# A first transform without its two zero columns, coupled ticks in the first pair, an earlier identity load, and evictions shared 5 to 4

## The chip, the cores and the metric

The kernel runs on one core of one Trainium2 chip. The metric is device time in microseconds (us), from the start of an execution to its end. Before the change the median of three runs is 385.36 us (384.66 to 386.22).

The names of the profile are used throughout: PE is the matrix engine, PEld its weight loads, DVE the vector engine, ACT the scalar engine, POOL and SP the two engines that here mostly issue DMAs. ps is PSUM, the memory that PE writes to, in eight banks of 512 float32 columns.

## The reference

Two layers follow each other. The first is a causal long convolution of x (8 x 5696 x 128) with h (5696 x 128) along the sequence, by FFT of twice the length; the second keeps 64 Fourier modes of the result, mixes their channels with a complex 128 x 128 matrix per mode, goes back, adds that to its input, and adds a ReLU of a 128 x 128 product:

```
Xf = np.fft.rfft(x, n=2*S, axis=1);  Hf = np.fft.rfft(h, n=2*S, axis=0)
x  = np.fft.irfft(Xf * Hf, n=2*S, axis=1)[:, :S, :]
X  = np.fft.rfft(x, axis=1)
Yr = einsum('bmd,mde->bme', Xr, w_r) - einsum('bmd,mde->bme', Xi, w_i)
Yi = einsum('bmd,mde->bme', Xr, w_i) + einsum('bmd,mde->bme', Xi, w_r)
u  = x + np.fft.irfft(Y, n=S, axis=1)
return u + np.maximum(u @ w_ch, 0.0)
```

## The kernel before

All transforms are matrix products on PE. The sequence of 5696 is cut into J = 64 columns of NQ = 89 rows, and NK = 90 frequencies k (0 to 89) come out of the first transform. The batch is worked in four pairs (g_ = 0 to 3, two sequences each).

**Order of the work.** Nothing is scheduled by a planner: a recorder writes the instructions of each engine down in the order of the calls in the source, and puts in the semaphore waits that the named tokens call for (reads, writes, and an extra list, `after`). So each engine, and each DMA queue, works strictly in the source's order, and whatever stands behind a waiting instruction of its queue waits too.

**First transform (`a_tile`, tiles j = 0 to 31).** Each tile takes four channels: four matmuls of a 128 x 128 slice of Xin against the constant F (f1_sb, 180 columns: real and imaginary part of each of the 90 frequencies). Their output, 4 x 180 float32 columns, fills two banks and is evicted to As (a_sb) with a scale, by DVE (line 317) or ACT (line 313). In As the group 2k + r of 128 columns holds the real (r = 0) or imaginary (r = 1) part of frequency k. The imaginary parts of k = 0 and of k = 89 are zero, and so are two columns of F, columns 1 and 179. h goes through the same transform once, in 16 tiles, into Ah.

For the first pair the 32 tiles are evicted by ACT and DVE in turn, with a filter tick of h between some of them; there are four PSUM slots of two banks. For the later pairs tiles 0 to 5, the border tiles, stand inside the last ticks of the pair before (`border`), and tiles 6 to 31 follow as a run: even tiles on ACT, odd ones on DVE, and tile 31 in halves, one on each engine. Matmuls of F with itself (`keep`, and 92 before the first tile) stand where PE would have nothing to do.

**Ticks.** A pair then has 23 ticks t of four frequencies (the last has two), numbered s in what follows when a later stage of the same tick is meant. For tick t, `second(t)` does the second transform, 16 matmuls of 64-row slices of As against M (k by k; real part, then imaginary part), into a slot of two banks. `products(t)` lets ACT copy the slot to Xs and DVE multiply it by the filter Hs into U (in the later pairs, for t = 3, 7, 11 and so on, DVE reads PSUM itself and ACT has no copy to make). Two ticks later four matmuls with the constants W1, W2 (`Wc`, 512 columns each) make Z, in two of three PSUM banks (4, 5 and 6), which ACT evicts to a slot Zs (or Zt); SP stores the slot to the DRAM scratch zscr, and a tick later short matmuls with G take the modes out of it. In the last pair the store and the modes of tick s use the z slot s for s below 10, and then slots 0 to 7 again: ticks 13 and 21 have slot 3, ticks 14 and 22 slot 4. ACT may write a slot again only when the store of its earlier tick has landed.

In pairs 1 to 3 an odd tick issues `second(t)` and `second(t + 1)` together (`twin`), a couple, and the work on PE is then: 32 matmuls of the second transform, Z, G, Z, G. In pair 0 each tick stands alone. Ticks 0 to 16 of pair 0 also carry the filter's second transform, six ticks ahead (`filter_tick`, LH = 6).

**Last stage.** During the ticks of pair 3, `early` issues loads on the POOL queue for the last stage: the mixing weights W, ZT0 to ZT3 (pieces of zscr), the constants S4a, S4b and IBs. After tick 14 it also issues one on SP: `load_id`, the 32 KB identity Id, which goes to memory that z slots 8 and 9 of the last pair use, so that it waits for these slots (`after=ZY`), their stores included. When the ticks are over, `u_z` does the first 16 matmuls of the inverse transform (ZT0 with S4a and S4b), `mix` does 128 small matmuls with W (16 columns each), the result is turned with eight transposes that read Id (line 824), and from then on inverse transforms (`u_tile`), the product with w_ch, ReLU, addition and stores alternate until the end.

Of the kernel before, what the change touches and what calls it, by code (L numbers as in the profile page):

```python
# [4 lines left out]
P = 128  # L5
# [118 lines left out]
def bass_long_conv_fft__then__afno_spectral_mix_kernel(nc, x, h, moe_w_r, moe_w_i, moe_w_ch, out):  # L124
# [3 lines left out]
    J = 64  # L128
# [13 lines left out]
    f1 = np.zeros((P, 2 * NK))  # L142
    f1[0:NQ] = np.stack([fwd.real, fwd.imag], axis=2).reshape(NQ, 2 * NK)
# [105 lines left out]
    f1_sb = at("F1", 2 * NK, F16, take(2 * NK * 2))  # L249
# [13 lines left out]
    assert 2 * S + 8 * ZP <= AW * 2  # L263
# [19 lines left out]
    id_sb = at("Id", P, F16, r_off[1])  # L283
# [63 lines left out]
    R.add("scalar", lambda e: e.copy(zf, ap(f1_sb, 2 * NK, J, P - J, 1, [[0, XW // 2]])), [("f1",)], [("xz",)])  # L347
# [69 lines left out]
    dma("sync", wc_sb[:, :], bass.AP(c_w, 0, [[3 * P, P], [1, 2 * P]]), "c", (), [("wc",)])  # L417

# [13 lines left out]
    for i in range(WARM):  # L432
        mm(pv(6 + i % 2, 0, [[1, 2 * NK]]), f1_sb[:, 0:P], f1_sb[:, :], True, True, [("f1",)], [bank(6 + i % 2)])
# [6 lines left out]
    for j in range(16):  # L440
        t = turns("h", [0, 2, 4])
        for i in range(4):
            d = 4 * j + i
            mm(pv(t + i // 2, (i % 2) * 2 * NK, [[1, 2 * NK]]),
               ap(hp_sb, 2 * J * HS, 0, P, d, [[HS, 2 * J]]), f1_sb[:, :], True, True,
               [("hz",), ("hp", d // DC), ("f1",)], [bank(t + i // 2)])
        for i in range(4 if j < 15 else 26):
            mm(pv(6 + i % 2, 0, [[1, 2 * NK]]), f1_sb[:, 0:P], f1_sb[:, :], True, True, [("f1",)], [bank(6 + i % 2)])
        evac(bass.AP(ah_sb, 4 * j, [[HW, P], [DH, 2 * NK], [2, 2], [1, 2]]),
             pv(t, 0, [[1, 2 * NK], [512, 2], [2 * NK, 2]]),  # L450
             [bank(t), bank(t + 1)], [("ah", j)], 1.0 / 64,
             eng="vector" if j in (3, 7) else "scalar")
        if j % 2:
            i = j // 2 % 2 * XC + j // 4
            x_place(i, bass.AP(x_all, i * XB, [[RA, NQ], [D, XN], [1, D]]), XR[i])
# [5 lines left out]
    def a_tile(j, slots, eng=None):  # L461
        t = turns("s", slots) if len(slots) > 1 else slots[0]
        for i in range(4):
            d = 4 * j + i
            mm(pv(t + i // 2, (i % 2) * 2 * NK, [[1, 2 * NK]]),
               ap(x_sb, XW, 0, P, d, [[XS, 2 * J]]), f1_sb[:, :], True, True,
               XIN + XZ + [("f1",)], [bank(t + i // 2)])
        if eng == "both":
            for i, e in enumerate(("vector", "scalar")):
                evac(bass.AP(a_sb, 4 * j + 2 * i, [[AW, P], [D, 2 * NK], [1, 2]]), pv(t + i, 0, [[1, 2 * NK], [2 * NK, 2]]),  # L470
                     [bank(t + i)], [("as", j + i)], 1.0 / 64, eng=e, after=once(("hp", j), HP))
            return
        evac(bass.AP(a_sb, 4 * j, [[AW, P], [D, 2 * NK], [2, 2], [1, 2]]),
             pv(t, 0, [[1, 2 * NK], [512, 2], [2 * NK, 2]]),
             [bank(t), bank(t + 1)], [("as", j)], 1.0 / 64, eng=eng, after=once(("hp", j), HP))


# [8 lines left out]
    def filter_tick(t, banks):  # L486
        n = len(ticks[t])
        hb = banks
        for i, k in enumerate(ticks[t]):
            for r in range(2):  # L490
                for dh in range(2):
                    mm(pv(hb[dh], i * DH, [[1, DH]]),
                       ap(m_sb, MW, J * dh, J, k * 3 * J + (J if r == 0 else 0) + dh * J, [[1, P]]),
                       ap(ah_sb, HW, J * dh, J, (2 * k + r) * DH, [[1, DH]]), r == 0, r == 1,
                       AHT + mtok(k) + [("ag", k)], [bank(hb[dh])])
# [54 lines left out]
    def load_s4(part):  # L550
# [9 lines left out]
             14: lambda: (load_id(), clear_zt(1)),  # L560
# [7 lines left out]
    def load_id():  # L568
        dma("sync", id_sb[:, :], bass.AP(c_w, 2 * P, [[3 * P, P], [1, P]]), "c", (), [("id",)], after=ZY)

# [4 lines left out]
    def keep(n, b0):  # L575
        for i in range(n):
            mm(pv(b0 + i % 2, 0, [[1, 2 * NK]]), f1_sb[:, 0:P], f1_sb[:, :], True, True, [("f1",)], [bank(b0 + i % 2)])
# [17 lines left out]
    def twin(g_, t):  # L595
        return g_ > 0 and t % 2 == 1
# [9 lines left out]
    def second(g_, t):  # L606
        sl = slot_of(g_, t)
        for i, k in enumerate(ticks[t]):
            for r in range(2):
                for b in range(2):  # L610
                    col = k * 3 * J + (J if r == 0 else 0) + b * J
                    mm(pv(sl + b, i * D, [[1, D]]),
                       ap(m_sb, MW, J * b, J, col, [[1, P]]),
                       ap(a_sb, AW, J * b, J, (2 * k + r) * D, [[1, D]]), r == 0, r == 1,
                       AST + mtok(k), [bank(sl + b)])
# [100 lines left out]
    FOUR = [0, 2, 4, 6]  # L716
    for j in range(32):
        a_tile(j, FOUR)
# [4 lines left out]
    for g_ in range(NP):  # L723
# [15 lines left out]
        if g_ + 1 < NP:  # L739
            for j in range(6, 32):  # L740
                a_tile(j, [(4, 6, 0, 2)[(j - 7) % 4] if j > 6 else 0], "both" if j == 31 else V if j % 2 else A)
# [99 lines left out]
    def o_tile(g_, b, r4):  # L841
# [29 lines left out]
        R.add("scalar", lambda e: e.activation(rv, src_r, RELU), bk, [("r", i % NR)], after=once(("r", i % NR), G_ALL + XTT + [("y", 0), ("y", 1), ("id",)]))  # L871
# [67 lines left out]
```

## Time and profile before

| | |
|---|---|
| Median of three runs | 385.36 us (384.66 to 386.22) |
| The profiled execution's own time | 387.21 us |
| Its span, first to last instruction | 385.1 us |
| PE / DVE / ACT / POOL busy | 362.4 / 296.6 / 314.3 / 85.2 us |
| Mean granted clock of PE | 0.98 |
| DMA | 103.94 MB, mean 270 GB/s |

Stages of the span, from a table of windows:

| us from the span's start | work |
|---|---|
| 0 to 27.1 | h and x loaded, h transformed |
| 27.1 to 43.5 | 32 tiles of pair 0 |
| 43.5 to 90.3 | ticks of pair 0 (from 81.4 on ticks 17 to 22, without the filter) |
| 90.3 to 106.8 | end of pair 0's ticks with border tiles, then the run of tiles 6 to 31 of pair 1 |
| 106.8 to 217.6 | the same for pairs 1 and 2, with their successors' tiles (145.8 to 162.2, 201.3 to 217.6) |
| 217.6 to 262.8 | ticks of pair 3 |
| 262.8 to 274.1 | start of the last stage: inverse transform, mix, transposes |
| 274.1 to 385.1 | the last stage |

A row of the table of instruction groups or of the timeline gives a start, a length, the engine, the source line, what it writes and reads, the shape and how many were merged; the part in brackets is the idle time before it and what ended it. Merged rows let the distance from one start to the next be worked out, which is shorter than the duration of one instruction, since the ends of instructions overlap with the next one's start. The chain of waits is read from the end of the execution back: at every step it goes to what released the instruction. PEclk is the share of its clock that PE was granted.

### The profile page before, as it was taken

What the parts mean: (1) busy time and instruction counts of PE and PEld (TensorE: products, weight loads), DVE (VectorE), ACT (ScalarE), POOL (GpSimd) and SP (SyncE); (2) the same over time, 40 slices, a digit from 0 to 9 for tenths busy, and PEclk for the clock granted to TensorE, in tenths of its full rate; (3) what the DMA queues carried; (4) which work ended last, traced back from release to release, by engine and by line L of the source; (5) the groups of instructions that cost most, each with busy time, mean ns of one, the idle gap of its engine ahead of it and who ended that gap; (6) DMA issues with size and microseconds to landing.
All of it is one profiled execution on the core that took longest, in us unless ns stands there. A gap on an engine that the chain in (4) does not pass through costs nothing.

```text
span 385.1 us, 12438 instructions
## 1 busy us (share of the span) xinstructions
PE 362.4 (94%) x5346; PEld 280.7 (73%) x5346; DVE 296.6 (77%) x336; ACT 314.3 (82%) x491; POOL 85.2 (22%) x134
## 2 busy tenths in 40 slices
PE   7989899999989999999999899978999999999994
PEld 7878766667856667756667666648789989888873
DVE  3649899988988998989999988761537767766665
ACT  8469699898989997899998899965447777688884
POOL 8812012100733311823203213307200000000000
PEclk9999999999999999999999999995799999999999
DMA  7999969977999995999995799999999999999877
GB/s 148 206 298 354 243 139 249 250 220 222 97 126 215 249 268 151 132 134 232 243 274 114 95 325 357 327 367 292 392 391 362 367 416 403 419 405 383 325 293 316
DMA packets 87137, 103.94 MB, mean 270 GB/s; under 512 B 22819, under 2 KB 72611, under 8 KB 83527
## 3 DMA queue, kind: packets, MB, share of 16 engines
q1 hardware_dynamic: 62603, 67.76, 50.7%
q0 software_dynamic: 24480, 35.40, 44.2%
q8 instruction: 42, 0.69, 0.7%
q14 instruction: 12, 0.10, 0.1%
HBM read 70.61 MB, written 51.12 MB: 316 GB/s over the span
## 4 chain that ended last, share of the span: by engine, by line
PE 76%; DMA 8%; DVE 6%; ACT 4%; POOL 3%; issue 2%; DVEq 0%; ACTq 0%; POOLq 0%
PE ps L323 76%; DMA Xr<-in_x_dram 4%; DMA zscr<-Zs 3%; DVE As L317 2%; DVE U L630 2%; POOL Xr L320 2%; ACT As L313 2%; ACT R L871 1%; POOL Hin L320 1%; DVE Xin L365 1%; DVE Hs L315 1%; ACT Zt L311 1%; ACT Zs L311 0%; DMA Hs<-Hs 0%; ACT Xs L311 0%
## 5 line engine op out<-in xcount | busy, mean ns | idle before, releaser
L323 PE MATMUL ps<-U,Wc 128*128 128x512 f16 (+1 forms) x368 | 94.4, 377 | 4.2 <-ACT Zs L311 3.7
L638 DVE TENSOR_TENSOR U<-Xs,Hs 128x2048 f16<-128x2048 f16 (+1 forms) x73 | 86.9, 1192 | 13.8 <-ACT Xs L311 13.1
L311 ACT CAST Xs<-ps 128x1024 f16<-128x1024 f32 (+1 forms) x77 | 75.1, 979 | 12.6 <-PE ps L323 7.6
L311 ACT CAST Zs<-ps 128x512 f16<-128x512 f32 (+1 forms) x132 | 69.3, 592 | 5.5 <-DMA zscr<-Zs 3.8
L872 DVE TENSOR_TENSOR O<-ps,R 128x512 f32<-128x512 f32 x81 | 52.3, 685 | 20.1 <-ACT R L871 11.2
L317 DVE TENSOR_SCALAR As<-ps 128x720 f16<-128x720 f32 x70 | 57.7, 886 | 5.2 <-PE ps L323 4.6
L871 ACT ACTIVATE R<-ps 128x512 f32<-128x512 f32 (+1 forms) x92 | 50.5, 591 | 8.5 <-PE ps L323 8.4
L323 PE MATMUL ps<-F,Xin 128*128 128x180 f16 x512 | 53.7, 249 | 3.9 <-DVE Xin L365 2.6
L323 PE MATMUL ps<-As,M 64*128 64x128 f16 x1440 | 50.3, 217 | 3.5 <-DVE U L630 2.9
L323 PEld LDWEIGHTS ps<-F,Xin 128*128 128x128 f16 x512 | 44.4, 155 | 12.6 <-DVE As L317 2.8
L323 PEld LDWEIGHTS ps<-U,Wc 128*128 128x128 f16 x368 | 28.6, 97 | 33.3 <-ACT Zs L311 7.6
L313 ACT ACTIVATE As<-ps 128x720 f16<-128x720 f32 (+1 forms) x61 | 45.7, 769 | 7.9 <-PE ps L323 6.5
L323 PE MATMUL ps<-WI,UT 128*128 128x256 f16 x360 | 51.1, 278 | 0.5 <-ACT UT L311 0.4
L311 ACT CAST UT<-ps 128x712 f16<-128x712 f32 x46 | 34.5, 752 | 19.2 <-PE ps L323 18.0
L323 PEld LDWEIGHTS ps<-As,M 64*128 64x128 f16 x1440 | 40.6, 94 | 9.7 <-DVE U L630 3.6
L323 PEld LDWEIGHTS ps<-WI,UT 128*128 128x128 f16 x360 | 39.1, 152 | 3.4 <-issue 1.8
L323 PE MATMUL ps<-IBs,C 128*128 128x356 f16 x128 | 40.3, 324 | 0.1
L320 POOL DMA_DIRECT2D Xt<-in_x_dram x40 | 21.1, 533 | 80.8 <-PE ps L323 80.3
L323 PEld LDWEIGHTS ps<-G,Zs 128*128 128x128 f16 x512 | 26.3, 97 | 14.3 <-ACT Zs L311 1.6
L638 DVE TENSOR_TENSOR U<-ps,Hs 128x2048 f16<-128x2048 f32 x15 | 34.3, 2284 | 0.0
L323 PE MATMUL ps<-G,Zs 128*128 128x128 f16 (+2 forms) x512 | 32.4, 193 | 0.0
L311 ACT CAST Zt<-ps 128x512 f16<-128x512 f32 x52 | 28.5, 624 | 0.3 <-PE ps L323 0.3
(88 smaller groups left out, 504.7 us busy)
## 6 DMA issues: line engine op xcount, KB each, us to landing
out_dram<-O SPq DMA_DIRECT2D x39, 512.0 KB, 7.6
zscr<-Zs SPq DMA_DIRECT2D x62, 256.0 KB, 7.0
zscr<-Zt SPq DMA_DIRECT2D x26, 256.0 KB, 6.8
Xt<-in_x_dram POOLq DMA_DIRECT2D x20, 320.0 KB, 7.1
W<-wscr POOLq DMA_DIRECT2D x4, 1024.0 KB, 8.2
M<-cM POOLq DMA_DIRECT2D x5, 720.0 KB, 16.9
ZT0a<-zscr SPq DMA_DIRECT2D x3, 1024.0 KB, 8.8
Hs<-Hs SPq DMA_DIRECT2D x44, 64.0 KB, 6.3
```

Source lines behind the costliest of these rows:

```text
L311: R.add(e, lambda h_: h_.copy(dst, src), reads, writes, after=after)
L313: R.add(e, lambda h_: h_.activation(dst, src, COPY, scale=scale), reads, writes, after=after)
L315: R.add(e, lambda h_: h_.tensor_copy(dst, src), reads, writes, after=after)
L317: R.add(e, lambda h_: h_.tensor_scalar_mul(dst, src, scale), reads, writes, after=after)
L320: R.add(eng, lambda h_: h_.dma_start(dst, src), reads, writes, ring=ring, after=after)
L323: R.add("tensor", lambda h_: h_.matmul(o, l, r, start=st, stop=sp), reads, writes)
L365: R.add("vector", lambda e: e.tensor_copy(bass.AP(x_sb, i * XN * XS, [[XW, NQ], [XS, XN], [1, D]]), src), list(toks) + XZ, [("xin", i)])
L630: R.add("vector", lambda e, b=b, s_=s_: e.tensor_tensor(bass.AP(u_s[i], b * 512, [[2048, P], [1024, 2], [1, n * D]]), s_, hv, MULT), [tok, ...
L638: R.add("vector", lambda e: e.tensor_tensor(uv, src, hv, MULT), bk + [("h", t, 0), ("h", t, 1, 0), ("h", t, 1, J)], [("u", i)])
L871: R.add("scalar", lambda e: e.activation(rv, src_r, RELU), bk, [("r", i % NR)], after=once(("r", i % NR), G_ALL + XTT + [("y", 0), ("y", 1 ...
L872: R.add("vector", lambda e: e.tensor_tensor(ov, src_u, rv, ADD), bk + [("r", i % NR)], [key + (h_,)], after=once(key, old))
```

## The change

Five things are changed.

1. F and everything made from it has 178 columns instead of 180 (`NF`): the two zero columns are left out. Groups 1 to 178 of As and Ah are written, and `group(k, r)` finds them; `parts_of(k)` leaves the imaginary part out for k = 0 and k = 89, so that `second` and `filter_tick` have two matmuls fewer for these k.
2. Id is put into group 179 of As, which nothing else writes now, and is loaded on SP at the very start, behind the other first constants (f1, SG, Wc). `load_id` and its place after tick 14 of pair 3 are gone, and so is one wait of the first ReLU.
3. `twin` also holds for ticks 17, 19 and 21 of pair 0: ticks 17 and 18, 19 and 20, 21 and 22 stand in couples.
4. The first pair's 32 tiles go to ACT and DVE by a list, `SHARE` (15 to DVE, 16 to ACT in the 31 first), and tile 31 is split between both.
5. In the runs of tiles 6 to 31, tiles 6 to 30 go to ACT and DVE in groups of nine, five to ACT and four to DVE: 14 and 11 instead of 13 and 12. The border tiles themselves, 0 to 5, are as before.

```
-    f1 = np.zeros((P, 2 * NK))
-    f1[0:NQ] = np.stack([fwd.real, fwd.imag], axis=2).reshape(NQ, 2 * NK)
+    NF = 2 * NK - 2
+    f1 = np.zeros((P, NF))
+    f1[0:NQ] = np.delete(np.stack([fwd.real, fwd.imag], axis=2).reshape(NQ, 2 * NK), [1, 2 * NK - 1], axis=1)
...
-    id_sb = at("Id", P, F16, r_off[1])
+    id_sb = at("Id", P, F16, a_as + (2 * NK - 1) * D * 2)
...
     dma("sync", wc_sb[:, :], bass.AP(c_w, 0, [[3 * P, P], [1, 2 * P]]), "c", (), [("wc",)])
+    dma("sync", id_sb[:, :], bass.AP(c_w, 2 * P, [[3 * P, P], [1, P]]), "c", (), [("id",)])
...
-            mm(pv(t + i // 2, (i % 2) * 2 * NK, [[1, 2 * NK]]),
+            mm(pv(t + i // 2, (i % 2) * NF, [[1, NF]]),
                ap(x_sb, XW, 0, P, d, [[XS, 2 * J]]), f1_sb[:, :], True, True,
...
-        evac(bass.AP(a_sb, 4 * j, [[AW, P], [D, 2 * NK], [2, 2], [1, 2]]),
-             pv(t, 0, [[1, 2 * NK], [512, 2], [2 * NK, 2]]),
+        evac(bass.AP(a_sb, D + 4 * j, [[AW, P], [D, NF], [2, 2], [1, 2]]),
+             pv(t, 0, [[1, NF], [512, 2], [NF, 2]]),
...
+    def group(k, r):
+        return 2 * k + r if k else 1
+
+    def parts_of(k):
+        return (0,) if k in (0, NK - 1) else (0, 1)
...
-            for r in range(2):
+            for r in parts_of(k):
...
-             14: lambda: (load_id(), clear_zt(1)),
+             14: lambda: clear_zt(1),
...
-    def load_id():
-        dma("sync", id_sb[:, :], bass.AP(c_w, 2 * P, [[3 * P, P], [1, P]]), "c", (), [("id",)], after=ZY)
...
     def twin(g_, t):
-        return g_ > 0 and t % 2 == 1
+        return t % 2 == 1 and (g_ > 0 or NT - LH <= t < NT - 1)
...
+    SHARE = [V if c_ == "V" else A for c_ in "VAVAAVAVAVAVAVAVAVAAVVAVAVAVAVA"]
     for j in range(32):
-        a_tile(j, FOUR)
+        a_tile(j, FOUR, "both" if j == 31 else SHARE[j])
...
-                a_tile(j, [(4, 6, 0, 2)[(j - 7) % 4] if j > 6 else 0], "both" if j == 31 else V if j % 2 else A)
+                a_tile(j, [(4, 6, 0, 2)[(j - 7) % 4] if j > 6 else 0], "both" if j == 31 else (A, V)[(j - 6) % 9 % 2])
```

## Prediction

> **What bounds the kernel now.** I read the page first. PE is busy nearly all the time, and its clock falls once, in slices 28 and 29 of 40:
>
> ```profile
> PE 362.4 (94%) x5346; PEld 280.7 (73%) x5346; DVE 296.6 (77%) x336; ACT 314.3 (82%) x491; POOL 85.2 (22%) x134
> ...
> PEclk9999999999999999999999999995799999999999
> ```
>
> The chain of waits has one long DMA in it, just before that dip:
>
> ```profile
> 247.86 13.02 DMA zscr<-Zs
> ...
> 260.96 0.60 ACT Zs L311
> 261.55 0.05 issue
> 261.60 8.21 PE ps L323 x182
> ```
>
> The waits of 238 to 264 us say what this cost: ACT waited 3.8 us for a store, PE 3.7 us for ACT.
>
> ```profile
> ACT Zs L311 <- DMA zscr<-Zs: 3.8, 1, 3.8
> PE ps L323 <- ACT Zs L311: 3.7, 1, 3.7
> ```
>
> Why that store was late stands in the timeline of SP and in SP's waits (243 to 262 us): no store left between 243.61 and 247.86, while the identity load waited 3.4 us for a z slot's store to land. ACT's timeline has the data ready long before: four evictions from 244.47 on, 0.48 apart, two for tick 13 and two for tick 14, so ready at 245.5 and 246.5.
>
> ```profile
> SPq L320 <- DMA zscr<-Zt: 3.4, 1, 3.4
> ```
> ```profile
> 243.61 0.36 SPq L320 DMA_DIRECT2D zscr<-Zs  x1
> 247.48 0.33 SPq L320 DMA_DIRECT2D Id<-cW  x1
> 247.86 0.44 SPq L320 DMA_DIRECT2D zscr<-Zs  x1
> ```
> ```profile
> 244.47 2.06 ACT L311 CAST Zs<-ps 128x512 f16<-128x512 f32 x4
> ```
>
> Then windows by stage (us, busy of PE, PEld, DVE, ACT and POOL, clock, DMA share, GB/s). In pair 0's last ticks ACT is busy 8.90 of 8.90 us, as PE is. From the stall on, PE runs 12.5 us at half clock.
>
> ```profile
> 81.40:90.30 8.90, 8.90 (x134) 5.59 (x133) 6.70 (x7) 8.90 (x16) 0.00 (x0) 1.00 0.73 215
> ...
> 257.50:261.60 4.10, 0.42 (x8) 0.14 (x5) 0.00 (x0) 0.64 (x2) 0.00 (x0) 0.85 0.89 276
> 261.60:274.10 12.50, 12.27 (x213) 10.82 (x214) 4.53 (x6) 6.37 (x9) 10.05 (x11) 0.50 1.03 345
> ```
>
> Last, two rows of the timeline for the eviction of a 720-column tile. Back to back on DVE five take 4.17 us, the last 0.90: a start every 0.82. Seven on ACT, in h's transform, take 4.74, the last 0.84: a start every 0.65.
>
> ```profile
> 152.53 4.17 DVE L317 TENSOR_SCALAR As<-ps 128x720 f16<-128x720 f32 x5 [0.20 <-PE ps L323]
> ```
> ```profile
> 19.57 4.74 ACT L313 ACTIVATE Ah<-ps 128x720 f16<-128x720 f32 x7
> ```
>
> **The identity load.** Without it SP stores tick 13 at 245.6 instead of 247.86, and tick 14 at 246.6 instead of 248.34. Tick 21 needs tick 13's slot, at 257.2. If the store still takes 13.0 us it lands at 258.6; if it takes the 8.0 of the two stores issued at 241.7 and 243.6, at 253.6. Tick 14's store, which tick 22 needs, lands at 259.9 at the latest. What is late next is S4a, for the first inverse transform, which started at 262.89: issued at 247.73, it took 10.9 us, to 258.6, and now has two stores of 256 KB ahead of it, 0.7 us each at 360 GB/s: 260.0. With no wait at all PE would be there at 262.9 - 3.7 = 259.2; with the slow stores at 260.9. I take 260.1: **2.8 us** (2.0 to 3.7). POOL's loads of ZT2 and ZT3, which wait for the stores of ticks 0 to 14 and left from 262.2 on, can now leave from about 256; S4a (247.7) and IBs (251.3) are queued before them, so they use DMA time that was idle around 261 (busy share 0.89) and delay neither.
>
> Then the clock. The 0.85 of the stall's window means half clock in its last 1.2 us, so the drop came at 260.4, 2.5 us after PE stopped (257.5 and its 0.42 us of work: 257.9). With a gap of about 1 us I expect none. At half clock, by starts in the timeline, the 55 inverse-transform matmuls up to 274.1 stand 74 ns apart (41 later), seven of IBs 296 (149), eight transposes 107 (the 128-column G matmuls of full clock: 55); mix, 30 ns, is no slower than G's short ones (27). That is 1.8 + 1.0 + 0.4 = 3.2 us, less 0.6 for two evictions in the middle (DVE 0.69, ACT 0.60) which eight matmuls then cover by 0.33 instead of 0.59. **2.6 us** (0 to 3.2).
>
> [...]
>
> **Its new place.** At the start the last x rows land at 26.24 on the chain, behind DMA. The 128 packets of Id are 8 an engine. The page's queue 1 has 62603 packets in 50.7% of 16 engines' span, 50 ns each, so at most 0.4 us, at least 0 if they fit in gaps: **+0.2**.
>
> **The runs of tiles.** PE needs 4 x 78 ns = 0.31 a tile, so evictions set the pace: before, DVE's 12 and a half, 12 x 0.82 = 9.8 us. After, 11 x 0.82 = 9.0 on DVE and 14 x 0.65 = 9.1 on ACT, 0.7 less. With four slots some is lost where two ACT tiles stand side by side: **0.4 a run, 1.2 in three**. If ACT's interval were its duration here, 0.78, the run would be 10.9: 1.1 longer each. I take 0.65, the row in which ACT was never out of work. Nothing waits longer for a tile: the first tick after a run needs all of them, whichever engine wrote them.
>
> **The first 32 tiles.** DVE has 16 evictions and one filter eviction (0.6), 13.6 of 15.4 us, and now half a tile less: 0.4, of which I take **0.3** (0 to 0.6). The 16 `keep` matmuls after the last tile move with it.
>
> **178 columns.** The nearest row is UT, 712 columns at an odd spacing too: 892 ns on DVE, 752 on ACT, against 901 and 781 for As. So 9 ns for each of some 60 evictions on the path: **0.5** (0 to 0.8). 576 matmuls shorter by 0.8 ns lie under the evictions; filler too. Of the 20 matmuls of k = 0 and 89 at 27 ns only the two at each pair's tick 0 hold up something, the first product: 4 x 0.05 = **0.2**.
>
> **The couples.** A couple takes PE 3.48 us in pair 3 (starts at 246.01 and 249.49), two single ticks here 3.70. But ACT's 0.90 + 0.48 + 0.48 a tick, 3.72, stay, in the same order, and ACT has no idle time: the product of tick 22, on which the border's DVE tiles wait, comes no earlier. **0** (0 to 0.7).
>
> Sum against the profiled execution (span 385.1, own time 387.21): 2.8 + 2.6 - 0.2 + 1.2 + 0.3 + 0.5 + 0.2 = 7.4, span 377.7, own time 379.8. The runs' median lies 1.85 below that execution, so 385.36 - 7.4 = **378.0**. The last stage gives nothing back: its PE waits for no DMA, and its ZT loads land 4.5 us or more ahead of use.
>
> **Rivals.**
> 1. The clock falls all the same during mix. For: at half clock it stayed there through 11 us of busy PE. Against: in 24.9 to 28.3 us PE was idle for 1.9 us and the clock stayed. [...]
> 2. The stall stays: the store is late for the bandwidth, not for SP, or another DMA takes its place for over 3 us. For: DMA share 0.89 to 1.03 around it, 13.3 us for the stores behind. Against: stores issued before 243.7 took 8. Then only 2.0 is left: 383.4. [...]
> 3. Slower: ACT becomes the bound of the runs. Without the runs' 1.2 the sum is 6.2, so three runs would have to be 2.1 longer each: 14 x 0.85 = 11.9 against 9.8. From 0.85 an eviction on it decides; measured are 0.65, and 0.78 from start to end. At 0.90 (12.6, 2.8 longer each) the kernel takes 385.4 + 8.4 - 6.2 = 387.6.
> 4. The zero columns do nothing where evictions cover them: 378.5, inside the first case.
>
> **How the numbers follow.** The first case 0.56 (376 to 380), rival 1 0.22, rival 2 0.13, rival 3 0.05, 0.04 for what I do not see. Range 375.0 to 383.8: below, S4a not late and the runs at 0.7; above, rival 2. About 0.5% (1.9 us) is what a measurement can tell: 383.4 is that bound, so rival 2 splits. Faster 0.84, same 0.08, slower 0.08.
>
> **What would show it.** Right: no wait of ACT for a zscr store in the last pair, SP's stores a tick apart there, PEclk 9 up to the last stage's end, the first use of S4a held up by its load alone, for about 1 us; evictions of the runs ending 0.5 us sooner; pair 0's couples with PE gaps on ACT. Wrong: a store of tick 13 still landing after 258, a 5 in PEclk, ACT starts in the runs over 0.75 apart, Xr landing over 0.4 us later.

## The result and the profile after

The changed kernel takes 387.17 us (median of 13 runs, 385.41 to 391.76); the kernel before, run beside it, 383.04 us (13 runs, 381.70 to 387.74). The ratio is 1.0095, 95% interval 1.0066 to 1.0124: slower by 1%, where 378.0, a faster kernel, was predicted. In a second comparison (e9 below, 6 runs) the ratio is 1.0135 (1.0084 to 1.0185). Ratios leave out runs over 1.5% above the fastest of their kernel (two of the changed kernel's 13 here); medians, ranges and the means of half-clock time below keep them. The profiled execution of the changed kernel takes 387.09 us, its span is 384.9.

The page of the profile of the changed kernel: 20 matmuls and 20 weight loads fewer, PE as busy as before, and a clock that falls twice.

```profile
PE 360.8 (94%) x5326; PEld 280.0 (73%) x5326; DVE 295.2 (77%) x333; ACT 314.3 (82%) x495; POOL 84.8 (22%) x134
...
PEclk9998999999999999999999999996799999999998
```

The 8 at the start is a half-clock stretch of 3.41 us from 27.72 on, in pair 0's first tiles; the 6 and 7 are 10.24 us from 263.24 on, where the kernel before had 13.65.

The chain of waits of the changed kernel (start, length, what) still has the long store, now tick 14's:

```profile
247.38 13.62 DMA zscr<-Zs
261.78 1.03 PE ps L324 x19
263.01 5.66 PE ps L324 x152
```

Its windows, for the end of pair 0's ticks, the stall, and the start of the last stage (us; busy of PE, PEld, DVE, ACT, POOL; clock, DMA share, GB/s):

```profile
81.40:90.30 8.90, 8.83 (x132) 5.59 (x132) 6.02 (x7) 7.99 (x14) 0.00 (x0) 1.00 0.65 189
259.50:261.80 2.30, 0.20 (x3) 0.12 (x3) 0.00 (x0) 0.65 (x2) 0.19 (x1) 1.00 1.04 315
261.80:273.50 11.70, 11.27 (x206) 9.79 (x207) 5.20 (x6) 5.57 (x6) 10.02 (x11) 0.56 1.02 355
```

So the stall is 2.0 us instead of 3.7, the half clock behind it is still there, and ACT is no longer busy all the time in pair 0's last ticks (7.99 of 8.90). SP and POOL in the timeline show what the stall hangs on now. SP is free of the identity load, as predicted:

```profile
246.40 0.36 SPq L321 DMA_DIRECT2D zscr<-Zs  x1
...
247.38 1.48 SPq L321 DMA_DIRECT2D zscr<-Zs  x1
...
247.49 0.54 POOL L321 DMA_DIRECT2D ZT1a<-zscr  x1 [0.82 <-PE ps L324]
248.02 0.54 POOL L321 DMA_DIRECT2D ZT1b<-zscr  x1
248.55 0.54 POOL L321 DMA_DIRECT2D S4a<-cS  x1
```

Tick 13's store (246.40) lands at 251.90, after 5.5 us. Tick 14's store is issued 0.11 us before ZT1a, its issue takes 1.48 us instead of 0.36, and it lands at 261.00, behind all three loads of POOL (255.52, 256.69, 258.69).

None of this explains a loss: by these rows the execution should be a little shorter than that of before, and it is, 387.09 against 387.21. But the profiled execution of before was 4 us over the median of its kernel, and that of the changed kernel is at its median. The table compares stages where nothing disturbs them (us between first matmuls, from traces without a dip or a stall in the stage). Stages also differ from one execution to the next by more than some of these rows do: over the 20 traces of this document the ticks of a middle pair take 39.0 to 40.4 us, those of pair 0 46.1 to 48.8 (the changed kernel's 47.07, and 48.03 in e9); of the middle pairs an undisturbed one is given.

| stage | before | 178 columns alone (e10) | changed kernel | what it shows |
|---|---|---|---|---|
| 32 tiles of pair 0 | 16.43 | 16.29 | 16.22 | 178 columns 0.14, sharing 0.07 |
| border to end of a run of tiles | 16.37 | 16.22 | 15.97 | 178 columns 0.15, sharing 5 to 4 0.25 |
| ticks of a middle pair | 39.07 | 39.01 | 39.06 | nothing |
| ticks of pair 0 | 46.3 to 46.9 | 46.14 | 47.07 | couples cost 0.7 (46.40 in e3, without them) |
| ticks of pair 3, without a stall | 41.27 | - | 41.22 | nothing |
| first inverse transform to first IBs matmul | 8.2 to 8.6 | 11.74 | 8.42, in e9 12.28 | see below |

All that the change was to do to evictions it did, 1.4 us together (0.14 + 0.07 + 3 x 0.40), less 0.7 for the couples. From tick 17's first matmul to the first border tile the couples show best: 11.57 to 11.61 us in seven of the eight traces that have them (13.24 in e7), 10.70 to 10.90 in eight of the twelve without (11.2 to 12.0 in the other four), so 0.7 to 0.9. What the change lost is elsewhere.

### The profile page after: what moved, and what is told of

The parts are those of the page before. It is cut to its first block, busy times and chain, and to the rows that moved or that the text cites. A ratio compares the mean times of both kernels' runs of the same rounds, so it can differ in the third digit from the quotient of the medians.

```text
span 384.9 us, 12401 instructions
## 1 busy us (share of the span) xinstructions
PE 360.8 (94%) x5326; PEld 280.0 (73%) x5326; DVE 295.2 (77%) x333; ACT 314.3 (82%) x495; POOL 84.8 (22%) x134
## 4 chain that ended last, share of the span: by engine, by line
PE 64%; DMA 12%; ACT 11%; DVE 6%; POOL 3%; issue 2%; DVEq 0%; ACTq 0%; POOLq 0%
PE ps L324 64%; ACT As L314 6%; DMA Xt<-in_x_dram 4%; DMA Xr<-in_x_dram 4%; DMA zscr<-Zs 4%; DVE As L318 2%; DVE U L635 2%; POOL Xr L321 2%; ACT Xs L312 1%; ACT R L877 1%; POOL Hin L321 1%; ACT Zs L312 1%; DVE U L643 1%; DVE Hs L316 1%; DVE Xin L366 1%
## 5 line engine op out<-in xcount | busy, mean ns | idle before, releaser
L878 DVE TENSOR_TENSOR O<-ps,R 128x512 f32<-128x512 f32 x81 | 52.3, 685 | 20.3 <-ACT R L877 11.2
L318 DVE TENSOR_SCALAR As<-ps 128x712 f16<-128x712 f32 (+1 forms) x67 | 55.3, 873 | 6.6 <-PE ps L324 5.1
L324 PE MATMUL ps<-F,Xin 128*128 128x178 f16 x512 | 53.1, 253 | 4.3 <-DVE Xin L366 2.9
L324 PEld LDWEIGHTS ps<-F,Xin 128*128 128x128 f16 x512 | 45.6, 155 | 11.5 <-DVE As L318 3.1
L314 ACT ACTIVATE As<-ps 128x712 f16<-128x712 f32 (+1 forms) x65 | 45.6, 761 | 8.5 <-PE ps L324 8.0
L324 PEld LDWEIGHTS ps<-G,Zs 128*128 128x128 f16 x512 | 26.1, 96 | 16.7 <-ACT Zs L312 4.2
```

Source lines behind the costliest of these rows:

```text
L314: R.add(e, lambda h_: h_.activation(dst, src, COPY, scale=scale), reads, writes, after=after)
L318: R.add(e, lambda h_: h_.tensor_scalar_mul(dst, src, scale), reads, writes, after=after)
L324: R.add("tensor", lambda h_: h_.matmul(o, l, r, start=st, stop=sp), reads, writes)
L878: R.add("vector", lambda e: e.tensor_tensor(ov, src_u, rv, ADD), bk + [("r", i % NR)], [key + (h_,)], after=once(key, old))
```

## The experiments

Half-clock time below is worked out from each run's span and mean granted clock, 2 x (1 - clock) x span (the share granted is 1.00 or 0.50 in the traces of the kernel before and of the changed one), and averaged over the runs of a kernel: 10.6 us in 47 runs of the kernel before on the chip of e1 to e4 (9.4 to 10.7 on the others), 14.3 in the changed kernel's 13. Ratios are to the kernel before, run on the same chip.

### Which part loses: e1 to e4

e1 is the kernel before, unchanged. It shows what identical kernels differ by.

> The kernel before, unchanged, to see how typical the profiled execution of before is (own time 387.21 against a median of 383.04 over 13 runs). Theory A, that the profiled execution had something that most do not (a stall of PE for a z slot, and with it the half clock of 260.4 to 274.1): the mean granted clock of most executions is 0.985 or more, spans near 380.5, and a profile of such a one shows no 3.7 us wait of PE for ACT Zs near 258. Theory B, that the stall is in every execution and the difference lies elsewhere (start, DMA): clocks near 0.980 in all, the wait of 3.7 us there again.

Measured: 385.65 us, ratio 1.0034 (0.9995 to 1.0073). Its trace differs from the other execution of the same code: the identity load left at 244.62, not 247.48, and tick 14's store landed at 261.50 all the same; stall 2.35 us.

e2 is the kernel before with the couples alone:

```
-        return g_ > 0 and t % 2 == 1
+        return t % 2 == 1 and (g_ > 0 or NT - LH <= t < NT - 1)
```

> The kernel before with the couples of pair 0 alone. Theory A, from the trace after, where PE stands before the second half of the first couple until DVE has evicted the last filter tick (81.42) and ACT idles 1.0 us: slower by 0.5 to 1.0 us, ACT busy about 8.0 of the 8.9 us after tick 17's start. Theory B, that the couples are neutral (as forecast) and the loss is from the rest: same within 0.2 us.

Measured: 384.56 us, ratio 1.0009 (0.9975 to 1.0042), an interval too wide to tell 0 from the 0.7 of the traces. Its last stage has the code of the kernel before, identity load included, and in this execution there is no stall at all: tick 14's store, issued at 247.31, lands at 253.59. So the stall that the prediction set out to remove comes in some executions of one kernel and not in others (of the five traces with before's code there, two have it: before and e1, not e2 and the later e6 and e14).

e3 is the changed kernel without the couples:

```
-        return t % 2 == 1 and (g_ > 0 or NT - LH <= t < NT - 1)
+        return g_ > 0 and t % 2 == 1
```

> The changed kernel without the couples of pair 0. Theory A: 0.5 to 1.0 us below the changed kernel (386.2 to 386.7 where that has 387.2), still above the kernel before. Theory B: as the changed kernel, 387.2. If the couples were the whole loss: as before, 383.0, or below.

Measured: 387.0 us, ratio 1.0064 (1.0028 to 1.0099). The couples are not what loses 1%.

e4 has the 178 columns and the early identity load, and nothing else of the change: e3 and

```
-        a_tile(j, FOUR, "both" if j == 31 else SHARE[j])
+        a_tile(j, FOUR)
...
-                a_tile(j, [(4, 6, 0, 2)[(j - 7) % 4] if j > 6 else 0], "both" if j == 31 else (A, V)[(j - 6) % 9 % 2])
+                a_tile(j, [(4, 6, 0, 2)[(j - 7) % 4] if j > 6 else 0], "both" if j == 31 else V if j % 2 else A)
```

> The kernel before with the 178 columns and the identity read at the start, nothing else (no couples, evictions shared as before). Theory A, that the early identity or the shorter transform carries most of the loss (Xr later by 0.2 us, a half clock in the first tiles, the store of tick 14 caught behind POOL's loads): 385 to 387, slower by 0.5 to 1.0%. Theory B, that they are harmless and the loss comes from couples and sharing: 382 to 383, same or 0.3% faster.

Measured: 388.46 us, ratio 1.0084 (1.0045 to 1.0123). The loss is in these two.

### A first theory: the gap before the first tile (e5, e6), and two remedies (e7, e8)

Theory A started from the extra dip at 27.7 us. The half-clock stretches inside the executions are 3.41, 6.83, 10.24 or 13.65 us long, multiples of 3.413 us, so I cut the executions into windows of that length, from the edges of these stretches. For each window I worked out how far the matmuls fill it: rows / 128 x columns, at 2.4 columns a ns (512-column matmuls start 215 ns apart), half of that at half clock (356-column matmuls start 296 ns apart there, 149 at full clock). The window in which PE waits for x, in the kernel before and in the changed one:

```profile
24.88:28.30 3.42, 1.54 (x21) 1.36 (x18) 1.36 (x3) 0.66 (x1) 0.77 (x2) 1.00 1.01 389
```
```profile
24.31:27.72 3.41, 1.44 (x19) 1.25 (x17) 1.38 (x2) 0.07 (x1) 0.03 (x1) 1.00 1.03 382
```

These are filled 0.38 and 0.35; the clock fell after the second. e5 closes the gap in the changed kernel, e6 widens it in the kernel before; e7 and e8 add to e5.

The filler behind h's last tile, in e5 (changed kernel) and in e6 (kernel before):

```
-        for i in range(4 if j < 15 else 26):
+        for i in range(4 if j < 15 else 46):
...
-        for i in range(4 if j < 15 else 26):
+        for i in range(4 if j < 15 else 22):
```

e7 is e5 and the first part of the next diff, e8 is e7 and the second part, together with six more such matmuls ahead of mix's evictions:

```
-             15: lambda: load_zt(1, "gpsimd"),
+             20: lambda: load_zt(1, "gpsimd"),
...
         for m in range(m0, m1):
+            if m % 4 == 3:
+                mm(pv(7 if m < 32 else 5, 0, [[1, NF]]), f1_sb[:, 0:P], f1_sb[:, :], True, True, ...)
```

> The changed kernel with 46 instead of 26 filler matmuls behind h's last tile: the 1.87 us in which PE waits for x (25.29 to 27.16 us) shrink to about 0.4. Theory A (what the change costs is, first, a half-clock window of 3.4 us in pair 0's first tiles: in the traces the clock fell after each window of 3.413 us in which rows x columns of the matmuls filled 0.36 of it or less, 0.35 in the changed kernel here, and stayed where they filled 0.38 or more, as in the kernel before): no half clock near 27 us, pair 0's first tick at 43.6 instead of 44.6, half-clock time by the runs' mean clock 14.3 us falls to about 11, median 385.5. Rival (the extra half clock lies at the last stage alone, the first window is chance): half-clock time stays about 14 us, median 387 within 0.8.

> The kernel before (180 columns, all else as it was) with 22 instead of 26 filler matmuls behind h's last tile: PE is idle 0.3 us longer there, as the 178 columns make it. Theory A: the window there is filled 0.29 to 0.32 instead of 0.38 to 0.40, so the clock falls in most runs: half-clock time from 10.6 us to 13 to 14, median 1.0 to 1.9 us over the kernel before. Rival: no difference, within 0.7 us of the kernel before.

> e5 and the load of ZT1 moved from after tick 15 to after tick 20 of the last pair, so that nothing of it is in the queues when ticks 13's and 14's stores leave. Theory B (these stores land 13.6 us after issue because the two halves of ZT1 and S4a, issued within 0.5 us of them, share the engines with them; in the trace of the couples alone the same store took 6.3): tick 14's store lands before 256, ACT does not wait for it, PE's idle of 2.0 us at 259.5 goes, the last half-clock stretch is 6.8 instead of 10.2 us; median 2.5 to 4 us under e5, 382 to 383. Rival (the bandwidth is full anyway): the store lands after 259 as before, or the loads of ZT1 to ZT3 come too late and PE waits for them from 270 on: e5's time or more.

> e7 and a dense filler matmul of 178 columns behind every eight thin ones of mix (16), and six where PE waits for mix's evictions. Theory A (a window is judged by rows x columns, not by whether PE has an instruction): the windows of mix are filled 0.45 or more instead of 0.31 to 0.36, no half clock before the tail; 16 x 0.075 = 1.2 us of PE more, 3.2 us of half clock less: 2 us under e7, about 380.5. Rival (PE counts as busy there anyway at over 0.9, the clock falls for another reason): the half clock stays and the time is 1.2 to 2.4 us over e7.

e5: 384.04 us, ratio 0.9968 (0.9922 to 1.0013), half-clock time 11.0. The loss is gone, as A said. e6: 383.16 us, ratio 0.9973 (0.9938 to 1.0009), half-clock time 9.8. Nothing is lost, against A. But e6 is a weak test: in its trace PE waits for x 1.87 us, in before's 1.88, since the end of h's transform moves by more than four fillers (0.3 us) from one execution to the next (e1 waits 1.78, e2 1.44). What tells against A are e9, e10 and e13 below; so e5 must heal something else.

e7: 383.88 us, ratio 0.9969 (0.9933 to 1.0006). The stall is gone, as theory B of its expectation has it. Ticks 13's and 14's stores leave as early as in the changed kernel:

```profile
246.28 1.34 SPq L321 DMA_DIRECT2D zscr<-Zs  x2
```

With only S4a issued near them (248.27) they land at 251.52 and 252.28, after 5.2 and 5.0 us, and ACT waits for neither. But the median is e5's, not 2.5 to 4 us less: probably since e5, too, has the stall in only part of its executions (the clocks of its runs go from 0.977 to 0.993).

e8: 382.26 us, ratio 0.9963 (0.9930 to 0.9995), half-clock time 3.0. In its trace the clock does not fall before PE's end. The same stage in e7 and in e8, two windows each:

```profile
258.29:261.70 3.41, 3.07 (x68) 2.57 (x66) 1.39 (x2) 2.98 (x6) 3.41 (x5) 1.00 0.91 297
261.70:265.11 3.41, 3.41 (x113) 3.41 (x110) 2.00 (x1) 1.71 (x2) 3.41 (x5) 1.00 1.04 423
```
```profile
257.58:260.99 3.41, 3.07 (x71) 2.78 (x70) 1.90 (x2) 2.98 (x5) 3.41 (x4) 1.00 1.05 407
260.99:264.40 3.41, 3.41 (x100) 3.41 (x97) 1.50 (x1) 1.21 (x2) 3.41 (x6) 1.00 1.03 424
```

PE is busy 3.41 of 3.41 us in both second windows. e7's is filled 0.31 and the clock falls behind it; e8's is filled 0.44 and it stays. So the busy time, which is the same, does not tell these two windows apart, and the fill does, as theory A said. By the medians the gain on e7 is 1.6 us of the 2 expected; by the ratios it is 0.2, and the two intervals overlap.

### What is lost: the changed kernel again, and 178 columns alone (e9, e10)

e9 is the changed kernel once more. e10 is the kernel before with 178 columns alone, that is e4 with the identity load where it was:

```
-    id_sb = at("Id", P, F16, a_as + (2 * NK - 1) * D * 2)
+    id_sb = at("Id", P, F16, r_off[1])
...
-             14: lambda: clear_zt(1),
+             14: lambda: (load_id(), clear_zt(1)),
```

> The changed kernel as it is, once more, beside the next three. Theory A: PE idle 1.9 us or more before pair 0's first tile, a half-clock window of 3.4 us behind it in most runs, and by the mean clocks 14 to 16 us of half clock (10.6 in the kernel before, 11.0 in e5): median 386 to 387.5, 0.6 to 1.2% over the kernel before. Rival (the first measurement, and e3 and e4, fell on a worse chip, and e5 on a better one): within 0.4% of the kernel before, half-clock time as e5's.

> The kernel before with 178 columns and nothing else of the change (the identity load after tick 14, no couples, tiles shared as before). Theory A (shorter filler and shorter h transform, not the identity load, open the gap before the first tile): half-clock time 13 to 16 us, median 1 to 2.5 us over the kernel before, as e4. Rival C (the early identity load is what costs, by the stores of ticks 13 and 14 leaving beside ZT1 in every run): 0.5 us under the kernel before, from the shorter evictions, half-clock time 10 to 12 us.

e9: 388.45 us, ratio 1.0135 (1.0084 to 1.0185). e10: 388.7 us, ratio 1.0109 (1.0054 to 1.0163); 6 runs each. The early identity load is cleared; the loss comes with the 178 columns. And neither trace has the dip near 27 us. What both have is a wait of PE in mix that nothing in the profile ends. The timeline of PE in e9:

```profile
263.04 0.97 PE L324 MATMUL ps<-XT,W 128*128 128x16 f16 x27
268.17 1.22 PE L324 MATMUL ps<-XT,W 128*128 128x16 f16 x37 [4.15 <-issue]
```

and the chain of e10:

```profile
260.51 4.04 PE ps L324 x107
264.55 3.10 issue
267.65 1.84 PE ps L324 x45
```

e3 has the same, 3.10 us. Counting all of PE's records (matmuls, weight loads, some hundred others) from 0 in the order of time, the idle time stands before number 7617 in all three. A second, smaller one of 0.8 to 1.1 us stands before number 8897, 5 x 256 later, in e4, e9 and e10. The profile's instruction queue has 42 packets with 0.69 MB, 16 KB each, and the changed kernel's PE has 10762 records, 256 a packet. So the two places stand whole packets apart, and I read the wait as PE out of code; e13 to e16 below test whether it goes with the place of the code. A block is here the 256 records from one such place to the next. In e9 the DMA queues over the 6.4 us after PE passed number 7361, and in the 1.1 us behind that (packets, MB, share):

```profile
q0 software_dynamic: 246, 1.69, 74.7%
q1 hardware_dynamic: 1241, 0.62, 32.0%
...
q0 software_dynamic: 56, 0.38, 84.7%
q1 hardware_dynamic: 57, 0.03, 8.7%
q8 instruction: 1, 0.02, 5.3%
```

The packet starts only at 265.71, lands at 266.65, and PE goes on at 268.17. In the traces of the kernel before and of the changed one, up to the last stage, the last packet to land ahead of a block starts from 1.0 us before PE's records enter the block before it to 4.6 us after that; in the kernel before the one ahead of number 7617 starts at 259.48, 2.24 us after PE passed 7361 (257.24). In e9 PE passes 7361 at 259.23, and POOL has just issued loads of 2.9 MB:

```profile
257.05 0.53 POOL L321 DMA_DIRECT2D ZT2a<-zscr  x1 [4.78 <-DVE U L643]
257.57 0.53 POOL L321 DMA_DIRECT2D ZT2b<-zscr  x1
258.09 0.54 POOL L321 DMA_DIRECT2D ZT3a<-zscr  x1
258.62 0.53 POOL L321 DMA_DIRECT2D ZT3b<-zscr  x1
```

Theory D: leaving out the zero columns takes 20 matmuls, 40 instructions, out of PE's program, four matmuls for each pair and for h; so number 7361 falls 5 instructions before the first matmul of the last stage, where it fell 45 before. There its packet meets the loads of ZT2 and ZT3, and the thin matmuls of mix, 27 to 29 ns apart, use up the block soon: PE goes from 7361 to 7617 in 5.06 us in the changed kernel, in 10.14, the stall included, in the kernel before. The 20 fillers of e5 put exactly those 40 instructions back.

### The code moved by itself (e13 to e16)

e11 and e12 ran beside e9 and e10 and are told further down. Four kernels separate A from D. The eight fillers at the end of each run of tiles are doubled or left out, which moves the code by 48 instructions and leaves the first gap alone:

```
-                    keep(8, 6)
+                    keep(16, 6)      e13: changed kernel     e16: e10 (178 columns alone)
+                    keep(0, 6)       e14: kernel before      e15: e5 (gap closed)
```

> The changed kernel with 16 instead of 8 filler matmuls at the end of each of the three runs of tiles, where PE is idle 0.86 us and eight take 0.6: 48 PE instructions more ahead of the last stage, so the block boundary 7361 lies 44 instructions before the stall as in the kernel before (36), while the gap before the first tile is as in the changed kernel. D: no idle of PE in mix without a releaser, half-clock time 10 to 12 us, the time of e5, 383.5 to 384.5 (0 to 0.4% under the kernel before). A: nothing changes, 387 to 388.

> The kernel before without the eight filler matmuls at the end of each run of tiles: 48 PE instructions fewer ahead of the last stage, so that boundary 7361 lies 12 instructions behind the stall, as in the changed kernel (4). 180 columns, first gap and everything else as before. D: it loses as the 178 columns do, a lag of 6 us for that block where no stall covers it and 3 to 4 us of PE idle in mix: 386 to 389, 0.8 to 1.4% over the kernel before. A: no difference, within 0.4%.

> e5 (no gap before the first tile) without the eight filler matmuls at the end of each run: boundary 7361 lies 12 instructions behind the stall again. D: the loss comes back, 386 to 388. A: e5's time, 384 to 384.5.

> e10 (178 columns alone) with 16 instead of 8 filler matmuls at the end of each run. D: the 1.1% go, and what is left is the shorter evictions and the missing matmuls: 0.3 to 0.8 us under the kernel before. A: as e10, 1.1% over it.

e13: 384.78 us, ratio 1.0039 (1.0002 to 1.0076), half-clock time 10.7. e14: 389.79 us, ratio 1.0140 (1.0086 to 1.0193). e15: 389.67 us, ratio 1.0181 (1.0115 to 1.0248). e16: 383.71 us, ratio 1.0007 (0.9970 to 1.0044). All four come out 0.3 to 1.8 us over D's numbers, but on D's side, and A's fail each time: the kernel before loses 1.4% when only its code is moved, and the changed kernel gets most of its loss back. e13 and e16 also pay for their filler: a run of tiles takes 16.25 us in e13 against 15.97, so 0.8 us or 0.2% in three. In e14 and e15 PE idles longer behind the runs (0.93 us in e15, 0.27 in the changed kernel, behind pair 1's), and in e15 the clock falls there once (110.65); that part of their loss is not the code's, and its size is not known. The four move the code by changing filler; none moves it with the work of PE left as it was.

The waits of PE in the last stage's start, in e14 and then in e13:

```profile
PE ps L323 <- issue: 1.5, 2, 1.3
```
```profile
PE ps L324 <- ACT Zs L312: 1.7, 1, 1.7
PE ps L830 <- issue: 0.2, 1, 0.2
PE ps L324 <- issue: 0.2, 1, 0.2
```

All kernels with the last stage as it was, by the place of number 7361 (instructions from it to the weight load of the first S4a matmul); lag is from PE's passing 7361 to the start of the packet:

| kernel | place | ratio to before | half clock, mean us | lag | stall + idle in mix, us |
|---|---|---|---|---|---|
| before | 45 | 1 | 10.6 | 2.2 | 3.7 + 0 |
| e1 | 45 | 1.0034 | 12.0 | 1.7 | 2.4 + 0 |
| e2 | 45 | 1.0009 | 9.7 | 2.4 | 0 + 0 |
| e5 | 45 | 0.9968 | 11.0 | 2.5 | 2.4 + 0 |
| e6 | 37 | 0.9973 | 9.8 | 3.3 | 0 + 0 |
| e13 | 53 | 1.0039 | 10.7 | 2.9 | 1.7 + 0 |
| e16 | 53 | 1.0007 | 9.9 | 3.2 | 0 + 0 |
| changed | 5 | 1.0095 | 14.3 | -0.2 | 2.0 + 0 |
| e9 (the same) | 5 | 1.0135 | 16.0 | 6.5 | 0 + 4.2 |
| e3 | 5 | 1.0064 | 16.1 | 6.1 | 3.4 + 3.1 |
| e4 | 5 | 1.0084 | 16.7 | -0.8 | 2.6 + 0 |
| e10 | 5 | 1.0109 | 14.0 | 5.9 | 1.8 + 3.1 |
| e14 | -3 | 1.0140 | 15.5 | 3.8 | 0 + 1.3 |
| e15 | -3 | 1.0181 | 17.4 | 5.8 | 0 + 3.2 |

The two groups do not overlap in their ratios (the intervals of e13 and e3 do). The two small lags in the lower one are executions with a stall, in which the packet left 0.05 and 0.65 us before POOL issued ZT2a (in e3 it left after it: stall and idle both). So at this place every execution that was traced loses: it has the stall, or it has none, and then the code is late. In the upper group an execution without the stall is simply 3 to 4 us shorter, and these are the 380 us spans that the changed kernel never shows (its shortest span is 383.2; the kernel before has 378.9).

Two things stay open. The first is what holds the packet. In e16, as in e3 and e10, POOL issued ZT2a just before PE passed 7361 (0.15 and 0.18 us); the packet started after 3.2 us there and after 5.9 and 6.1 here. That the loads delay it is read from the queues of e9 and not tested by itself; what the runs show is that the loss comes and goes with the place of the code. The second is the rest of the last stage: from the first IBs matmul to the end the upper group takes 113.2 to 113.7 us, the lower 113.9 to 117.4. So 0.2 to 4 us of the loss lie behind mix. In e4, e9 and e10 the second wait is 0.8 to 1.1 of it, and in e4, whose mix has no wait, longer last stores add 1.9; the remainder is not explained.

### What the change is worth without the disturbances (e11, e12, e17, e18)

e11 is the kernel before with e8's three edits (the diffs above). e12 is e8 without the couples (e3's diff). e17 is e12 without the filler in mix, e18 keeps ten of its 16:

```
-            if m % 4 == 3:
+            if m >= 24 and m % 4 == 3:
```

> The kernel before with what e8 adds: 46 filler matmuls, ZT1 loaded after tick 20, filler in mix; the five parts of the change are not in it. With the clock and the stall out of the way the difference to e8 is what the change itself is worth: by the traces 3 x 0.35 (runs of tiles) + 0.3 (first 32 tiles) + 0.5 and 0.2 (178 columns) - 0.5 (couples) = 1.5 us, so 383.8 here if e8 is 382.3 again. Rival (the change's own parts are worth nothing, and only the clock differs): 382.3 within 0.5. No stall of PE before the inverse transform, no half clock before the tail in either case.

> e8 without the couples of pair 0: by the change's trace couples cost 0.5 us (PE waits 0.8 us for the filter eviction at 80.7, ACT is out of work for 0.9 us), by the run of the couples alone 0.9 at equal clock: 381.4 to 381.8 if e8 is 382.3. Rival (the order in pair 0 makes no difference): 382.3 within 0.3.

> e12 without the filler in mix. By the fill of the windows (0.31 to 0.36 in mix) the clock falls for one or two windows in every run: half-clock time 6 to 9 us by the mean clocks, against 2.0 in e12. If half clock there costs what the prediction put on it (2.6 us for the stage), 1 to 1.5 us over e12 (1.2 us of filler less); if the stage is bound by the 27 to 29 ns between thin matmuls, which half clock does not change, the same as e12 within 0.5 us.

> e12 with ten of the 16 filler matmuls in mix (from m = 24 on). The windows are filled about 0.39 to 0.42, just over the 0.38 under which the clock fell in all traces: half-clock time as in e12 in most runs, 6 x 0.076 = 0.45 us of PE less, 0.3 to 0.5 us under e12. If the window falls in a part that is filled under 0.38, half-clock time 5 to 6 us and the time of e12 or e17.

e11: 382.77 us, ratio 0.9956 (0.9924 to 0.9989). e12: 381.73 us, ratio 0.9945 (0.9914 to 0.9977), half-clock time 2.0. Run on one chip, the change without its couples is worth 1.0 us (0.4 to 1.6, worked out from the 12 runs of each). With its couples (e8, on another chip) it is worth 0.5 of the 1.5 us expected; e12 against e8 is 0.5 us less, too little to tell. e17: 381.88 us, ratio 0.9930 (0.9900 to 0.9959), half-clock time 8.0, so the time of e12 in spite of the half clock, the second case of its expectation. e18: 383.19 us, ratio 0.9970 (0.9940 to 1.0000), half-clock time 5.1: ten fillers are not enough in every run, and it is no better than e12, so its expectation failed. e17's PEclk shows no slice under 9 before the end, though one window of 3.41 us is at half clock (263.78):

```profile
PEclk9999999999999999999999999999999999999998
```

From the first inverse transform to the twenty-first IBs matmul e17 takes 16.18 us, e12, at full clock with all its filler, 16.78. Both beat the kernel before and the changed one; by them the filler in mix is worth nothing net. So the useful edits are 178 columns and the two sharings, with 20 more filler matmuls at the start and ZT1 loaded after tick 20; the early identity load is in these kernels too, but nothing shows a gain from it alone.

## Why the prediction was wrong, step by step

**What bounds the kernel.** This is where it began. The rows were read rightly, but they were those of one execution: stall 3.7 us, half clock 13.65 us. Of five traces with that code three have no stall. The prediction took what differs from one execution to the next for a property of the kernel, and put 5.4 of its 7.4 us on it. The median that it subtracted from, 385.36, was that of three runs; 13 give 383.04.

**The identity load, 2.8 (2.0 to 3.7).** SP was indeed free, and tick 13's store landed at 251.90, earlier than either value given. Tick 14's landed at 261.00, over the bound "259.9 at the latest", with ZT1 in the queues beside it (without, in e7, it took 5.0 us): rival 2, in one of the changed kernel's two traces. In the other the stall is gone, and 4.15 us of idle stand in mix instead. e4 against e10 gives the early load no measurable value, and its place does not settle whether a store is late: in the 13 traces besides before's that load ZT1 after tick 15, tick 14's store is issued 0.11 or 0.12 us ahead of ZT1a. It landed after 4.7 to 8.7 us in six (e2, e6, e14, e16; with the early load e9, e15) and after 13.3 to 15.0 in seven (e1, e10; with the early load the changed kernel, e3, e4, e5, e13). What removes the stall is e7's edit. The changed kernel's store was issued first and landed last; what held it, and why its issue took 1.48 us, stays open. The 360 GB/s that the step puts on a store of 256 KB is near what the kernel before's DMA moved from 245 to 260 us: 351, at a busy share of 1.04.

**The clock, 2.6 (0 to 3.2).** Rival 1 was right: the clock falls by or in mix with or without a stall, in all 16 traces without filler in mix (without a stall, for example, in e2, e6, e7, e16 and e17). The row that the prediction gave rival 1 for, half clock in spite of 12.27 of 12.50 us busy, was the right one to trust. No run shows that the clock stays up behind a stall of 1 us, on which the 2.6 rests; with the shortest one, 1.7 us in e13, it fell. The window that ended at 260.40, ahead of the drop, was idle for 2.5 of its 3.41 us, not for all of it, and filled 0.18. The size was too large also without that: from before's 17.62 us (first inverse transform to twenty-first IBs matmul, 11.2 us of it at half clock) to e17's 16.18 (3.4) are 1.4 us.

**Id's new place, +0.2.** x lands at 26.40 us, in all traces between 26.07 and 26.52: not to be told from nothing.

**The runs of tiles, 0.4 each.** Right in mechanism: ACT is now the bound, its tiles start (7.43 - 0.78) / 10 = 0.67 apart in the chain of the changed kernel:

```profile
100.42 7.43 ACT As L314 x11
```

The run is 0.40 shorter, of which the 178 columns have 0.15 (counted under their own heading) and the sharing 0.25. **The first 32 tiles, 0.3:** 0.07 from the sharing, 0.14 from the columns. Here the half-clock window of 27.7 us, in four of the twelve traces with that gap and not foreseen, costs 1.0 us where it comes (17.4 against 16.3 or so).

**178 columns, 0.5 and 0.2.** As evictions they gave 3 x 0.15 + 0.14 = 0.6, and e16, with its 1.0 us of extra filler taken off (runs of tiles 16.55 against 16.22), lies about 0.7 us under the kernel before: the size that was predicted, though the interval is wider than that. What the step left out is its other effect: "576 matmuls shorter" and a few missing were costed as time on PE alone, and not as 40 instructions that move all code behind them. That is what turned the sign, 3 to 5 us by the changed kernel against e13 and e10 against e16 with their extra filler taken off, and none of the rivals had it. What the start of a block costs differs: PE is idle 0.45 us before number 1985 in the kernel before and 0.23 before 9665 in the changed one, 1.3 (e14) to 4.2 us (e9) in mix, and 0.8 to 1.1 before 8897 (e4, e9, e10).

**The couples, 0 (0 to 0.7).** They lose 0.7 to 0.9. The last filter tick uses banks 2 and 3, and the first couple needs them: PE waits for DVE, and an ACT that was never idle becomes idle. From the changed kernel's timeline:

```profile
81.47 0.62 PE L324 MATMUL ps<-As,M 64*128 64x128 f16 x16 [0.77 <-DVE Hs L316]
...
82.67 1.07 ACT L312 CAST Zs<-ps 128x512 f16<-128x512 f32 x2 [0.91 <-PE ps L324]
```

**The rivals.** The one on the slow side, ACT as bound with 0.85 us an eviction, did not happen. What happened was 1, in every trace without filler in mix, 2 in part of the executions, and a third thing that was not listed: a wait in mix that comes and goes with the place of the code.

## What to carry to other kernels

Before a stall is costed, find out whether it belongs to the kernel or to one execution: here two of five traces of one code had it, and the mean clocks of e5's runs went from 0.977 to 0.993. Removing a few of an engine's thousands of instructions moves all code behind them: here 40 of PE's 10802 records brought number 7361 from 45 to 5 instructions ahead of the last stage, behind a burst of loads and ahead of mix's short matmuls, and that cost more than the edit saves. Idle time with no releaser before the same number in three traces (7617, in e3, e9 and e10) pointed at it, and a few filler instructions elsewhere (e13 to e16) tested it. A part that measures slower may be a good part in a bad place.

## What the runs showed of the hardware

- The instruction queue moved 42 packets with 0.69 MB, 16 KB each, for PE's 10802 records in the kernel before and 10762 in the changed one. In these two traces a packet took 0.88 to 1.71 us. The last one to land ahead of a block started, up to the last stage, from 1.0 us before PE's records entered the block before to 4.6 us after that, and in the middle of the last stage (numbers 9153 to 10433) 4.0 to 7.0 us after it, where PE took 8.7 to 9.9 us for a block. In e3, e9, e10, e14 and e15, where PE waited in mix, it started 3.8 to 6.5 us after PE passed 7361. PE went on 1.29 us after the packet's end where it was idle before number 1985 (the kernel before), 1.31 before 9665 (the changed kernel) and 1.52 before 7617 (e9).
- The clock fell behind windows of 3.41 us that the matmuls filled 0.18 (the kernel before, 256.99), 0.19 and 0.35 (the changed kernel, 259.83 and 24.31) and 0.31 (e7, 261.70), and stayed behind those filled 0.38 (the kernel before, 24.88) and 0.44 (e8, 260.99). At half clock it came back behind windows filled, at half rate, 0.94 (the kernel before, 270.64), 0.99 and 0.95 (the changed kernel, 27.72 and 270.07), and stayed low behind five filled 0.54 to 0.64 in the same two traces. In e7's window PE was busy 3.41 of 3.41 us. What decides it between these numbers is not shown; the 0.36 and 0.38 in the expectations of e5 and e18 were readings of such windows.
- Tick 14's store of 256 KB, issued 0.1 us before three loads of together 2.2 MB on another queue, landed after 4.7 to 8.7 us in six executions, and after 13.3 to 15.0 in seven, the same code on both sides (e2 and e6 against e1). What decides it was not found.
- The last stores took 5.3 us in e4 and 3.3 in e1, which makes its tail 1.9 us longer. The cause is not known.
